# An attention and feed-forward block: products with V in two halves of 64 rows, and the banks shared out anew

## The chip, the cores and the metric

The kernel runs on one core of one Trainium2 chip. The metric is the time of one execution on the device in microseconds (us), as the median of the runs. The core's engines work side by side, each through a list of its own in order: TensorE (PE in the profile, with its weight loads as PEld), VectorE (DVE), ScalarE (ACT), GpSimd (POOL) and SyncE (SP), which here only starts transfers. Matmul results land in PSUM, which has eight banks of 128 partitions x 512 fp32.

## What is computed

One transformer block on x of 2048 x 512 in fp32: 32 query heads of width 16 that share one key head and one value head, then a gated feed-forward part of width 1792.

```python
def _A_ref(x, wq, wk, wv, wo):
    q = (x @ wq).reshape(B, S, H, Dh).transpose(0, 2, 1, 3)
    k = x @ wk
    v = x @ wv
    scores = jnp.einsum("bhqd,bkd->bhqk", q, k) * (Dh ** -0.5)
    p = softmax(scores, axis=-1)
    o = jnp.einsum("bhqk,bkd->bhqd", p, v)
    return o.transpose(0, 2, 1, 3).reshape(B, S, H * Dh) @ wo

def _B_ref(x, w_gate, w_up, w_down):
    return (gelu(x @ w_gate) * (x @ w_up)) @ w_down

h = x + _A_ref(layernorm(x), wq, wk, wv, wo)
h2 = h + _B_ref(layernorm(h), w_gate, w_up, w_down)
```

## The kernel before

**Blocks and groups.** The 2048 query positions are cut into four blocks of 512 (T). Heads go in eight groups of four per block, and keys in 16 chunks of 128. One *step* of attention is one block, one group and one key chunk: 4 x 8 x 16 = 512 steps. A step has two halves (u), each for two heads.

**Scores.** `scores` (line 345) multiplies, for each half, the keys with the queries of two heads. Queries and keys are split into a high and a low part, so that a contraction has 50 rows; the two heads of a half lie in rows 0 to 49 and 64 to 113 of TensorE, which takes both matmuls at once as two tiles of 64 rows. Each writes one bank, so a half needs a pair of banks. One exponential on ScalarE (line 356) then takes the pair, 128 x 1024 elements, into the tile p. There are 1024 halves.

**Products with V.** `weigh` (line 358) runs when both halves of a step have been through the exponential: four calls, one per head, each with all 128 key rows of v_sb and 32 output columns, into four strips of 32 partitions of one accumulator bank, acc. The four strips are four tiles of 128 rows x 32 columns. After 16 chunks `evacuate` (line 371) copies acc to oT on VectorE; the copy then goes through DRAM, is divided by the sums (the upper half of each strip) and becomes the input of the output projection. These are the only products that TensorE takes in full fp32; the others use a rounded fp32 form with explicit high and low parts.

**Dense products.** The output projection, gate, up and down products of blocks 0 to 2 are cut by contraction rows as well: `rows(a)` (line 753) makes two streams, one over rows 0 to 63 and one over rows 64 to 127 of every product, and `step` (line 782) issues one matmul of each. The second stream runs LAG = 6 steps behind the first. A product has 12 matmuls in most cases. At its start a stream takes a bank from the list `spare`, and after the last matmul it gives the bank back to the end of that list and has VectorE read it (`done`: lines 585, 588, 635, 639, 702). The tile framework makes the next writer of a bank wait for the last reader. `queue_products` (line 722) lists the products: for each of blocks 0 to 2 four projections, 28 gate and up products, 8 down products of the runs of features and 4 more, and 4 of the block before where there is one.

**Order of work.** TensorE, ScalarE and GpSimd run in the order written. Three parts matter:

- In the *first stretch* (bank set `ps_first`), block 0's attention runs beside the query projections of the later blocks (`project_q`, line 195). The string PERIOD, played eight times, sets the order: s is a half of scores, v one V step, p a few matmuls of the projection, n a small piece of the same. There are three pairs of score banks: two called s in the pool pss, and a third, s3, for every third half (lines 347 to 349). One bank, d, serves the projections, and one is acc.
- In the *second stretch* (`ps_rest`), from half 279 on, the rounds of CYCLES (line 48) set it. A cycle starts with a burst of three or two V steps (`finish(count)`, line 1102) and then plays a string of s and d, d being a step of the dense streams. Two pairs of score banks, acc, and three dense banks d0, d1, d2 fill PSUM. `turn` (line 593) transposes the normed rows of a block, four transposes into a bank taken from `spare`, which VectorE reads twice.
- The *last part* (`last_dense`, line 818) does block 3's dense work alone, with banks of a new pool (`tail_bank`, line 792) in place of the score banks.

```python
PERIOD = "psssvvssvnsspsssvvssvnssvssvssvvssspssvssvvnsssvvssvss"
LAG = 6
CYCLES = (
    (3, "ssdddddsdddsddds", "vssvssvs"),
    (3, "ssdddddsdddsddds", "vssvssvs"),
    (2, "ssdddddsdddsdddsddds", "ssvssvss"),
)
```

Of the kernel before, what the change touches and what calls it, by code (L numbers as in the profile page):

```python
# [9 lines left out]
F32 = mybir.dt.float32  # L10
# [4 lines left out]
ALU = mybir.AluOpType  # L15
# [4 lines left out]
P = 128  # L20
# [37 lines left out]
def kernel(  # L58
# [12 lines left out]
    nc = tc.nc  # L71
# [6 lines left out]
    T = 512  # L78
    NT = S // P
    NB = S // T  # L80
    TB = T // P
    DC = D // P
    FC = F // P
    NG = H // 4
    KC = S // P
# [25 lines left out]
    v_sb = const.tile([P, KC, 2 * DH], F32, name="v_sb")  # L111
# [9 lines left out]
    def split(eng_hi, hi, lo, src, eng_lo=None):  # L121
        if eng_hi is nc.scalar:
            nc.scalar.activation(hi, src, AF.Copy)
        else:
            eng_hi.tensor_copy(hi, src)
        (eng_lo or nc.vector).tensor_tensor(lo, src, hi.bitcast(F32), op=ALU.subtract)
# [29 lines left out]
    def run(outer, first):  # L156
        banks, held_banks = ExitStack(), ExitStack()
        ps = pss = None
# [6 lines left out]
        width = 0  # L165

        def psum1(name):
            if not spare:
                return ps.tile([P, T], F32, tag="d", bufs=width, name=name)
            tag, bank = take_bank(name)  # L170
            spare.append(tag)
            return bank

        spare = []

        def take_bank(name):
            tag = spare.pop(0)
            return tag, ps.tile([P, T], F32, tag=tag, bufs=1, name=name)
# [143 lines left out]
        if first:  # L322
            set_banks("ps_pro")
            width = 8
# [19 lines left out]

        def scores(i, p, qg, kc, u):

            third = width == 1 and (2 * i + u) % 3 == 2
            pool, tag, bufs = (ps, "s3", 1) if third else (pss, "s", 2)
            s = pool.tile([P, 2, T], F32, tag=tag, bufs=bufs, name=f"s_{i}_{u}")
            for a in range(2):  # L350
                rows = slice(64 * a, 64 * a + KR)
                nc.tensor.matmul(  # L352
                    s[:, a, :], kaug[rows, kc * P : (kc + 1) * P], qg[rows, u, :],
                    start=True, stop=True,
                )
            nc.scalar.activation(p[:, 2 * u : 2 * u + 2, :], s, AF.Exp, scale=SCALE)  # L356

        def weigh(acc, p, kc):
            for j in range(4):
                nc.tensor.matmul(  # L360
                    acc[32 * j : 32 * j + 32, :], v_sb[:, kc, :], p[:, j, :],
                    start=(kc == 0), stop=(kc == KC - 1), skip_group_check=True,
                )

        def take_out():
            for step in outs.pop(0):
                step()

        def evacuate(b, g, acc):
            oT = sb.tile([P, T], F32, tag="oT", bufs=1, name=f"oT_{b}_{g}")
            nc.vector.tensor_copy(oT, acc)  # L373
            c, k = divmod(g, 2)
            if k == 0:
                pair[0] = sb.tile([P, 2, T], F32, tag="oc", bufs=2, name=f"oc_{b}_{c}")
            oc = pair[0]

            def move_out():
                for half in (1, 0):  # L380
                    for j in range(4):
                        r0, r1 = 64 * k + DH * j, 32 * j + DH * half
                        (nc.sync, nc.scalar)[j % 2].dma_start(
                            oc[r0 : r0 + DH, half, :], oT[r1 : r1 + DH, :]
                        )

            def turn_out():
                view = acc_d[:, g % 4, :].rearrange("(j s e) t -> j e s t", s=2, e=DH)
                for j in range(4):
                    r0 = 64 * k + DH * j  # L390
                    nc.sync.dma_start(oc[r0 : r0 + DH, :, :], view[j])


            def invert(t):
                sl = slice(t * P, (t + 1) * P)
                nc.vector.reciprocal(oc[:, 1, sl], oc[:, 1, sl])  # L396

            def divide():
                if c == 0:
                    o_blk[b] = [  # L400
                        sb.tile([P, DC, T], F32R, tag=f"o_{w}", bufs=1, name=f"o_{w}_{b}")
                        for w in ("hi", "lo")
                    ]
                hi, lo = o_blk[b]
                nc.vector.tensor_tensor(oc[:, 0, :], oc[:, 0, :], oc[:, 1, :], op=ALU.mult)
                split(nc.vector, hi[:, c, :], lo[:, c, :], oc[:, 0, :])


            def piece(t):
                sl = slice(t * P, (t + 1) * P)  # L410
                hi, lo = o_blk[b]
                invert(t)
                nc.vector.tensor_tensor(
                    oc[:, 0, sl], oc[:, 0, sl], oc[:, 1, sl], op=ALU.mult
                )
                split(nc.vector, hi[:, c, sl], lo[:, c, sl], oc[:, 0, sl])
                pieces[b] = t + 1

            if b == NB - 1 and g == NG - 1:
                move_out()  # L420
            else:
                nc.sync.dma_start(acc_d[:, g % 4, :], oT)
                if b == 0 and g < NG - 1:
                    outs.append([turn_out])
                else:
                    turn_out()
            if b == NB - 1 and g == NG - 1:
                last_out.append(piece)
            elif b > 0 and g == NG - 1:
                outs.extend([partial(piece, t), partial(piece, t + 1)] for t in (0, 2))  # L430
            elif k == 1:

                outs.extend([[] for _ in range(4 if b == 0 else 1)])
                outs.extend([partial(invert, t), partial(invert, t + 1)] for t in (0, 2))
                outs.append([divide])
            if b == 0 and g == NG - 1:
                while outs:
                    take_out()
                pieces[b] = TB
# [97 lines left out]
        def new_xT(b):  # L537
            xTs[b] = [
                db.tile([P, DC, T], F32R, tag=f"x2{w[0]}", bufs=1, name=f"x2{w[0]}_{b}")
                for w in ("hi", "lo")  # L540
            ]
# [49 lines left out]
            return f"pp_{b}_{t}", 3 * DC, terms, done, lambda: pieces.get(b, 0) > t  # L591

        def turn(b, t):
            tag, bank = take_bank(f"pxt_{b}_{t}")
            pt = bank.rearrange("p (c q) -> p c q", c=DC)
            xn = xbs.pop((b, t))
            for c in range(DC):
                nc.tensor.transpose(pt[:, c, :], xn[:, c * P : (c + 1) * P], ident)
            if b not in xTs:
                new_xT(b)  # L600
            sl = slice(t * P, (t + 1) * P)
            hi, lo = (x[:, :, sl] for x in xTs[b])
            nc.vector.tensor_copy(hi, pt)
            nc.vector.tensor_tensor(lo, pt, hi.bitcast(F32), op=ALU.subtract)
            spare.append(tag)
            load_x(b * TB + t + 3)
            turned[b] = t + 1

# [181 lines left out]
                ahead -= 1  # L790

        def tail_bank(name):
            return tail_ps.tile([P, T], F32, tag="t", bufs=5, name=name)

        tail_ps = None

# [21 lines left out]
        def last_dense():  # L818
            b = NB - 1
# [5 lines left out]
            def x_turn(t):  # L825
# [9 lines left out]
            xp, xn, h = (  # L835
                sb.tile([P, TB, D], F32, tag="p", bufs=PB, name=f"{n}p_{b}")
                for n in ("x", "xn", "h")
            )
# [2 lines left out]
            for j in range(2):  # L841
                load_w2(b, j)

            pps = [psum1(f"pp_{b}_0")]
            pps.extend(tail_bank(f"pp_{b}_{t}") for t in range(1, TB))

            def add_x(t):
                nc.tensor.matmul(pps[t], ident, xp[:, t, :], start=False, stop=False)
# [108 lines left out]
        acc = None  # L957
# [17 lines left out]
        def score(n):  # L975

            nonlocal acc
            i, u = divmod(n, 2)
            b, r = divmod(i, PER)
            g, kc = divmod(r, KC)  # L980
            if u == 0:
                if kc == 0:
                    cur["qg"] = qgs.pop((b, g))
                    acc = pss.tile([P, T], F32, tag="acc", bufs=1, name=f"acc_{b}_{g}")
                if kc == 2 and b * NG + g + 1 < NB * NG:
                    key = divmod(b * NG + g + 1, NG)
                    qgs[key] = load_q(*key)
                cur["p"] = sb.tile([P, 4, T], F32, tag="p", bufs=PB, name=f"p_{i}")
            scores(i, cur["p"], cur["qg"], kc, u)
            if u == 1:  # L990
                pend.append((b, g, kc, cur["p"], acc, n))

        banks.close()
        pss = held_banks.enter_context(
            tc.tile_pool(name="ps_s", bufs=1, side="right", space=PSUM)
        )
        set_banks("ps_first")
        width = 1


        n, lead = 0, 2 * PER + 23
# [55 lines left out]
                    finish(len(pend) - 2)  # L1057
        assert not outs
        set_banks("ps_rest")
        width = 3  # L1060
        spare.extend(f"d{i}" for i in range(width))

        def catch_up():
# [26 lines left out]
        for i in range(-((lead - end) // 16)):  # L1090
# [27 lines left out]
        tail_ps = outer.enter_context(  # L1118
            tc.tile_pool(name="ps_tail", bufs=1, side="right", space=PSUM)
        )  # L1120
# [335 lines left out]
```

## Time and profile before

| What | Value |
|---|---|
| time, median of 2 runs | 1413.44 us (1412.52 to 1414.37) |
| the profiled execution, its own time | 1410.17 us |
| its span in the trace | 1408.5 us |
| granted TensorE clock, mean | 0.999 |
| TensorE busy | 1387.5 us |
| ScalarE busy | 1030.1 us |
| VectorE busy | 630.8 us |

The profile is of one execution, and everything in it is measured from the start of its span. Busy time is time in which an instruction of the engine runs; a matmul's end is modelled, so rows of matmuls overlap, and the distance from start to start tells more than the length of a row. A row of a timeline merges neighbouring instructions of one kind: it gives the first start, the time from there to the last end, and after x the count. What stands in brackets is idle time before the row and what ended it. Waits of TensorE often stand at the weight load (PEld) that comes ahead of the matmul. A matmul in full fp32 leaves two records. A form like 64*128 gives the rows and columns of TensorE that a matmul takes.

### The profile page before, as it was taken

The page shows a single profiled execution, that of the slowest core. Times are in us where ns is not written, and L with a number is a line of the kernel's source. Part 1 is how long each engine was busy: PE and PEld are TensorE (multiplying, and loading weights), DVE is VectorE, ACT ScalarE, POOL GpSimd, SP SyncE. Part 2 cuts the span into 40 slices and gives each one's busy share as a digit, 9 for nine tenths or more (in the row PEclk, how much of TensorE's full clock was granted, in tenths as well). Part 3 has the DMA queues.
Part 4 walks back from the last instruction along what each step waited for, and adds up shares of the span by engine and source line. Part 5 has one row for each costly group of instructions (what it writes and reads, how often), then busy time and mean ns, then how long its engine had stood idle before and what let it go on. Part 6 is the DMA issues. An engine that isn't in the chain of part 4 may idle for free.

```text
span 1408.5 us, 25209 instructions
## 1 busy us (share of the span) xinstructions
PE 1387.5 (99%) x10435; PEld 752.5 (53%) x10435; DVE 630.8 (45%) x1027; ACT 1030.1 (73%) x1147; POOL 222.1 (16%) x321
## 2 busy tenths in 40 slices
PE   8999999999999999999999999999999999999998
PEld 6433333325455555545555555545555555557886
DVE  7411231314364444454354444445264453537665
ACT  7799999997877777877777777777778777752000
POOL 6575777731000000000000000000000000001000
PEclk9999999999999999999999999999999999999999
DMA  4465676745222333321432333311423333344352
GB/s 160 154 198 182 230 243 203 241 137 195 80 95 76 113 113 103 103 71 51 162 104 80 132 102 102 105 62 36 149 95 102 118 102 105 102 142 176 128 191 77
DMA packets 66851, 180.31 MB, mean 128 GB/s; under 512 B 9484, under 2 KB 9484, under 8 KB 66696
## 3 DMA queue, kind: packets, MB, share of 16 engines
q1 hardware_dynamic: 55712, 144.33, 30.8%
q0 software_dynamic: 9760, 34.08, 7.4%
q8 instruction: 84, 1.38, 0.4%
q10 hardware_dynamic: 1256, 0.20, 0.1%
q14 instruction: 39, 0.32, 0.1%
HBM read 130.87 MB, written 47.45 MB: 127 GB/s over the span
## 4 chain that ended last, share of the span: by engine, by line
PE 93%; DMA 2%; ACT 2%; DVE 1%; issue 1%; POOL 0%; SPq 0%; DVEq 0%; ACTq 0%
PE acc L360 33%; PE s L352 20%; PE pg L772 8%; PE pu L772 8%; PE pd L772 8%; PE pq L205 3%; PE pd L802 3%; PE pu L802 3%; PE pg L802 3%; PE pp L772 2%; ACT p L356 2%; DMA w<-w_d 1%; PE pk L1235 1%; DMA x<-in_A_x_dram 1%; PE pd_rest L814 1%
## 5 line engine op out<-in xcount | busy, mean ns | idle before, releaser
L356 ACT ACTIVATE p<-s 128x1024 f32<-128x1024 f32 x1024 | 959.7, 1040 | 227.8 <-PE s L352 225.0
L360 PE MATMUL acc<-p,v_sb 128*32 128x512 f32 x4096 | 490.0, 598 | 0.0
L352 PE MATMUL s<-qg,kaug 50*128 50x512 f32 x1984 | 383.7, 425 | 4.3 <-ACT p L356 4.2
L352 PEld LDWEIGHTS s<-qg,kaug 50*128 50x128 f32 x1984 | 169.5, 184 | 286.6 <-ACT p L356 136.4
L360 PEld LDWEIGHTS acc<-p,v_sb 128*32 128x32 f32 x4096 | 109.9, 109 | 228.6 <-issue 220.5
L772 PE MATMUL pg<-x2h,w 64*128 64x512 f32 x672 | 173.8, 391 | 0.0
L772 PE MATMUL pu<-x2h,w 64*128 64x512 f32 x672 | 172.7, 391 | 0.0
L135 POOL TENSOR_SCALAR rstd<-mv 128x1 f32<-128x1 f32 x16 | 3.5, 219 | 964.2 <-DVE mv L133 964.0
L772 PE MATMUL pd<-w,gh 64*128 64x512 f32 x624 | 123.7, 392 | 1.4 <-DVE h L702 1.4
L702 DVE TENSOR_TENSOR h<-h,pd 128x512 f32<-128x512 f32 x80 | 54.4, 687 | 147.9 <-PE pd L772 147.9
L772 PEld LDWEIGHTS pg<-x2h,w 64*128 64x128 f32 x672 | 94.3, 185 | 12.0
L772 PEld LDWEIGHTS pu<-x2h,w 64*128 64x128 f32 x672 | 94.2, 186 | 11.5
L772 PE MATMUL pg<-x2l,w 64*128 64x512 f32 x336 | 99.3, 391 | 0.0
L772 PE MATMUL pu<-x2l,w 64*128 64x512 f32 x336 | 99.0, 392 | 0.0
L772 PEld LDWEIGHTS pd<-w,gh 64*128 64x128 f32 x624 | 68.1, 185 | 13.1 <-DVE h L702 2.7
L911 ACT ACTIVATE ga<-ga 128x512 f32<-128x512 f32 x14 | 8.8, 632 | 89.6 <-DVE ga L908 89.6
L373 DVE COPY oT<-acc 128x512 f32<-128x512 f32 x32 | 22.1, 691 | 110.7 <-PE acc L360 110.5
L772 PE MATMUL pd<-w,gl 64*128 64x512 f32 x312 | 71.5, 391 | 0.0
L639 DVE TENSOR_TENSOR g<-g,pg 128x512 f32<-128x512 f32 x42 | 28.8, 686 | 90.1 <-PE pg L772 90.1
L396 DVE RECIPROCAL oc<-oc 128x128 f32<-128x128 f32 x64 | 56.6, 922 | 23.3 <-DMA oc<-acc_d 17.5
L635 DVE COPY g<-pg 128x512 f32<-128x512 f32 x42 | 29.1, 692 | 72.0 <-PE pg L772 72.0
L639 DVE TENSOR_TENSOR u<-u,pu 128x512 f32<-128x512 f32 x42 | 28.8, 686 | 68.3 <-PE pu L772 68.3
(247 smaller groups left out, 1465.5 us busy)
## 6 DMA issues: line engine op xcount, KB each, us to landing
w<-w_d SPq DMA_DIRECT2D x112, 512.0 KB
w<-w_d SPq DMA_DIRECT2D x28, 1024.0 KB
qg<-q_d SPq DMA_DIRECT2D x62, 200.0 KB
q_d<-qh SPq DMA_DIRECT2D x32, 256.0 KB
acc_d<-oT SPq DMA_DIRECT2D x31, 256.0 KB
oc<-acc_d SPq DMA_DIRECT2D x124, 64.0 KB
w_d<-w_0b POOLq DMA_DIRECT2D x14, 512.0 KB, 4.3
w_d<-w_1b POOLq DMA_DIRECT2D x14, 512.0 KB, 3.3
```

The lines of the kernel that those rows point to most:

```text
L205: nc.tensor.matmul(pq, wt[c][:, d, :], xt[:, d, :], start=(n == 0), stop=(n == 3 * DC - 1),)
L352: nc.tensor.matmul(s[:, a, :], kaug[rows, kc * P : (kc + 1) * P], qg[rows, u, :], start=True, stop=True,)
L356: nc.scalar.activation(p[:, 2 * u : 2 * u + 2, :], s, AF.Exp, scale=SCALE)
L360: nc.tensor.matmul(acc[32 * j : 32 * j + 32, :], v_sb[:, kc, :], p[:, j, :], start=(kc == 0), stop=(kc == KC - 1), skip_group_check=True,)
L373: nc.vector.tensor_copy(oT, acc)
L396: nc.vector.reciprocal(oc[:, 1, sl], oc[:, 1, sl])
L635: nc.vector.tensor_copy(half, bank)
L639: nc.vector.tensor_tensor(half, half, bank, op=ALU.add)
L702: nc.vector.tensor_tensor(hs[b, t], hs[b, t], bank, op=ALU.add)
L772: nc.tensor.matmul(bank, lhsT[r], rhs[r], start=(k == 0), stop=(k == n - 1), skip_group_check=True,)
L802: nc.tensor.matmul(bank, lhsT, rhs, start=(i == 0), stop=(i == len(ts) - 1))
L814: nc.tensor.matmul(bank, lhsT, rhs, start=(i == 0), stop=(i == len(ts) - 1))
```

## The change

`weigh` makes two calls per head instead of one, on key rows 0 to 63 and 64 to 127, so eight tiles of 64 rows x 32 columns instead of four of 128 x 32. The calls on the upper rows and on the lower rows go into accumulators of their own, acc[0] and acc[1], each one bank. `evacuate` copies the first to oT and adds the second. PSUM's eight banks are shared out anew: the third pair of score banks in the first stretch is gone, and the projections there have two banks (width = 2) instead of one; in the second stretch the dense streams have two banks instead of three, and `turn` takes half of a score pair instead of a dense bank. The last part has six banks in its pool instead of five, and its first projection takes one of these. The strings that set the order, LAG and the list of products stay as they are.

```diff
         def scores(i, p, qg, kc, u):
 
-            third = width == 1 and (2 * i + u) % 3 == 2
-            pool, tag, bufs = (ps, "s3", 1) if third else (pss, "s", 2)
-            s = pool.tile([P, 2, T], F32, tag=tag, bufs=bufs, name=f"s_{i}_{u}")
+            s = pss.tile([P, 2, T], F32, tag="s", bufs=2, name=f"s_{i}_{u}")
...
         def weigh(acc, p, kc):
             for j in range(4):
-                nc.tensor.matmul(
-                    acc[32 * j : 32 * j + 32, :], v_sb[:, kc, :], p[:, j, :],
-                    start=(kc == 0), stop=(kc == KC - 1), skip_group_check=True,
-                )
+                for h in range(2):
+                    half = slice(64 * h, 64 * h + 64)
+                    nc.tensor.matmul(
+                        acc[h][32 * j : 32 * j + 32, :], v_sb[half, kc, :], p[half, j, :],
+                        start=(kc == 0), stop=(kc == KC - 1), skip_group_check=True,
+                    )
...
             oT = sb.tile([P, T], F32, tag="oT", bufs=1, name=f"oT_{b}_{g}")
-            nc.vector.tensor_copy(oT, acc)
+            nc.vector.tensor_copy(oT, acc[0])
+            nc.vector.tensor_tensor(oT, oT, acc[1], op=ALU.add)
...
         def turn(b, t):
-            tag, bank = take_bank(f"pxt_{b}_{t}")
-            pt = bank.rearrange("p (c q) -> p c q", c=DC)
+            bank = pss.tile([P, 2, T], F32, tag="s", bufs=2, name=f"pxt_{b}_{t}")
+            pt = bank[:, 0, :].rearrange("p (c q) -> p c q", c=DC)
...
-            spare.append(tag)
...
         def tail_bank(name):
-            return tail_ps.tile([P, T], F32, tag="t", bufs=5, name=name)
+            return tail_ps.tile([P, T], F32, tag="t", bufs=6, name=name)
...
-            pps = [psum1(f"pp_{b}_0")]
-            pps.extend(tail_bank(f"pp_{b}_{t}") for t in range(1, TB))
+            pps = [tail_bank(f"pp_{b}_{t}") for t in range(TB)]
...
-                    acc = pss.tile([P, T], F32, tag="acc", bufs=1, name=f"acc_{b}_{g}")
+                    acc = [
+                        pss.tile([P, T], F32, tag=f"acc{h}", bufs=1, name=f"acc{h}_{b}_{g}")
+                        for h in range(2)
+                    ]
...
         set_banks("ps_first")
-        width = 1
+        width = 2
...
         set_banks("ps_rest")
-        width = 3
+        width = 2
         spare.extend(f"d{i}" for i in range(width))
```

## Prediction

> **What bounds the kernel now.** I read the page's busy rows first, then the chain, the costliest groups, and then a table of stretches cut where the kernel changes its way of working.
>
> ```profile
> span 1408.5 us, 25209 instructions
> PE 1387.5 (99%) x10435; PEld 752.5 (53%) x10435; DVE 630.8 (45%) x1027; ACT 1030.1 (73%) x1147; POOL 222.1 (16%) x321
> ...
> PE 93%; DMA 2%; ACT 2%; DVE 1%; issue 1%; POOL 0%; SPq 0%; DVEq 0%; ACTq 0%
> ...
> L356 ACT ACTIVATE p<-s 128x1024 f32<-128x1024 f32 x1024 | 959.7, 1040 | 227.8 <-PE s L352 225.0
> L360 PE MATMUL acc<-p,v_sb 128*32 128x512 f32 x4096 | 490.0, 598 | 0.0
> ...
> L373 DVE COPY oT<-acc 128x512 f32<-128x512 f32 x32 | 22.1, 691 | 110.7 <-PE acc L360 110.5
> ```
>
> ```profile
> 49.70:320.50 270.80, 266.94 (x1831) 98.18 (x1831) 64.48 (x91) 260.78 (x279) 173.91 (x213) 1.00 0.64 207
> 320.50:1258.80 938.30, 934.61 (x7747) 507.06 (x7744) 440.48 (x703) 720.23 (x787) 10.08 (x25) 1.00 0.30 102
> ```
>
> The columns of the second fence are stretch, length, then busy us of PE, weight load, DVE, ACT, POOL, then clock and DMA. TensorE works through (99% busy, 93% of the chain), so whatever makes it wait is paid in full. The first stretch (block 0's attention, set ps_first, scores 0 to 279) is bound twice over: TensorE 266.94 and ScalarE 260.78 of 270.80 us. In the second (set ps_rest: attention woven with dense products) ScalarE and VectorE have slack and TensorE has none.
>
> **The change, part by part.** I take the products with V first, then the two exchanges of banks that pay for their second accumulator, then the small edits.
>
> *Products with V.* 2048 calls leave 4096 records, so each fp32 call is two passes. The burst below is three V steps, 24 records, six times four passes side by side.
>
> ```profile
> 687.63 0.40 PE L772 MATMUL pu<-x2h,w 64*128 64x512 f32 x2
> 687.87 0.39 PE L352 MATMUL s<-qg,kaug 50*128 50x512 f32 x2
> 688.19 2.78 PE L360 MATMUL acc<-p,v_sb 128*32 128x512 f32 x24
> 690.90 0.73 PE L352 MATMUL s<-qg,kaug 50*128 50x512 f32 x4
> ```
>
> 490.0 us over 1024 rounds of four is 0.48 with the transitions; I take 0.43 for a pass, six of which are 2.58 of the 2.71 us from burst to score. The change doubles the calls and halves their rows. A pass still streams 512 columns, so nothing is gained if all eight tiles run side by side, and that is my value: 0. A 64-row pass is not shorter as such, which the rows below exclude as a gain: 64-row products follow each other by 0.23 (697.32 to 697.55), 128-row ones by 0.24 (39.08 to 39.32). The loss ends at the two halves running in turn, 512 steps x 0.86 = 440 us; the nearest rows (the paired 64-row products, the four V passes at once) speak for 0.
>
> That the passes may overtake each other is read from the burst: a V step takes two pass times (0.86 us), though each of its four calls holds two passes of one tile in sequence. In strict program order it would take four pass times now (high, low with the next high, and so on) and eight after the change, 512 x 4 x 0.43 = 880 us more. In the Trainium skill, "TensorE: Matmul & The Clock Gate", section "Part 3: Packing small matmuls — row/col tiling", matmuls start and end strictly in program order; by that rule the sum below would be 2565 us, and the trace disagrees with it here (0.86 us a step, not 1.72).
>
> *The transitions.* What the burst pays for entering and leaving: 687.87 to 688.19 is 0.32 against 0.24 between a product and a score; 2.71 against 2.58; and the second score after it comes 0.33 after the first (690.90 + 0.73 - 0.40) instead of 0.24. Together 0.08 + 0.13 + 0.09 = 0.30 us a burst. The code has 8 x 11 bursts in the first stretch and 47 x 3 in the second, 229: 69 us. The change makes the row count alike (64) on both sides and leaves the column count different (32 against 128). Rows where only one of the two differs:
>
> ```profile
> 39.08 0.40 PE L1235 MATMUL pk<-xT_lo,wk_hi 128*128 128x512 f32 x1
> 39.32 0.39 PE L1235 MATMUL pk<-xT_hi,wk_lo 128*128 128x512 f32 x1
> 39.64 0.39 PE L243 MATMUL pqn<-qs,sel 128*32 128x512 bf16 x1
> 39.96 0.50 PE L205 MATMUL pq<-xT_hi,wq_hi 128*128 128x512 f32 x1
> ```
>
> ```profile
> 138.61 0.40 PE L205 MATMUL pq<-xT_hi,wq_lo 128*128 128x512 f32 x1
> 138.93 0.30 PEld L352 LDWEIGHTS s<-qg,kaug 50*128 50x128 f32 x4 [0.36 <-issue]
> 138.93 0.50 PE L352 MATMUL s<-qg,kaug 50*128 50x512 f32 x2
> ```
>
> Columns alone (128 to 32 and back, 39.32, 39.64, 39.96): 0.32 each, against 0.24. Rows alone (138.61 to 138.93): 0.32. Both (687.87 to 688.19): 0.32. The three cost the same, so taking the row half away saves nothing. Value 0, end -69.
>
> *Two dense banks instead of three.* Two streams of products run six steps apart, each holding one bank for 12 matmuls. With three banks the stream that ends a product takes the third. With two, the bank that it just gave back is the only one free, so its next matmul waits for VectorE, and everything behind it on TensorE's queue (the other stream, scores, V) waits too.
>
> ```profile
> 696.88 0.69 DVE L373 COPY oT<-acc 128x512 f32<-128x512 f32 x1 [2.84 <-PE acc L360]
> ...
> 697.32 0.39 PE L772 MATMUL pg<-x2h,w 64*128 64x512 f32 x2
> ...
> 697.55 0.39 PE L772 MATMUL pu<-x2h,w 64*128 64x512 f32 x1
> ...
> 697.74 0.69 DVE L635 COPY g<-pg 128x512 f32<-128x512 f32 x1 [0.17 <-PE pg L772]
> ```
>
> The product pg ends with the matmul of 697.32, its bank is read from 697.74 to 698.43, and the next product pu starts at 697.55 in another bank. One place of this trace already has too few banks:
>
> ```profile
> 933.68 0.39 PE L772 MATMUL pd<-w,gl 64*128 64x512 f32 x2
> 933.91 0.39 PE L772 MATMUL pd<-w,gh 64*128 64x512 f32 x1
> 934.11 1.28 DVE L702 TENSOR_TENSOR h<-h,pd 128x512 f32<-128x512 f32 x2 [3.46 <-PE pd L772]
> 934.85 0.29 PEld L772 LDWEIGHTS pd<-w,gh 64*128 64x128 f32 x3 [0.98 <-DVE h L702]
> 934.85 0.72 PE L772 MATMUL pd<-w,gh 64*128 64x512 f32 x3 [0.55 <-DVE h L702]
> ```
>
> The last matmul starts at 933.68, VectorE at 934.11 (0.43 later), the first of two reads ends near 934.79, the next product starts at 934.85 (0.06 later): 1.17 from the last matmul to the next product, 0.94 more than the usual 0.23. So a handover costs 0.94, and 0.71 where a score (0.23) stands in between.
>
> ```profile
> L702 DVE TENSOR_TENSOR h<-h,pd 128x512 f32<-128x512 f32 x80 | 54.4, 687 | 147.9 <-PE pd L772 147.9
> L635 DVE COPY g<-pg 128x512 f32<-128x512 f32 x42 | 29.1, 692 | 72.0 <-PE pg L772 72.0
> ```
>
> How many: the list holds 3 x (4 + 28 + 8 + 4) + 4 = 136 products, two halves each, 272 handovers (80 of them are the L702 row, 42 the L635 row). A round of the three cycles has 36 steps, so one stream ends products after steps 12, 24 and 36, the other after 6, 18 and 30. Step 36 is followed by a V burst, as 687.63 to 690.90 shows, and that covers the 1.17; step 30 by a score; the other four by the next step. So 5/6 of 272 = 227 handovers at (4 x 0.94 + 0.71)/5 = 0.89: **203 us**. Low end: all at 0.71, 161 us. High end: VectorE is busy 440.48 of 938.30 us, so on average 0.47 x half of 0.69 = 0.16 us more before a read begins, 240 us. I take 203, by the handover that was measured.
>
> *Two pairs of score banks in the first stretch instead of three.* A score waits for the exponential two scores back, not three.
>
> ```profile
> 130.49 0.73 PE L352 MATMUL s<-qg,kaug 50*128 50x512 f32 x4
> ...
> 132.15 0.73 PE L352 MATMUL s<-qg,kaug 50*128 50x512 f32 x4
> ...
> 133.80 0.87 PE L352 MATMUL s<-qg,kaug 50*128 50x512 f32 x4
> ...
> 136.45 0.96 PE L352 MATMUL s<-qg,kaug 50*128 50x512 f32 x6
> ...
> 137.05 2.86 ACT L356 ACTIVATE p<-s 128x1024 f32<-128x1024 f32 x3 [0.18 <-PE s L352]
> ```
>
> An exponential takes 260.78/279 = 0.93 us, and the one after an empty ScalarE starts 0.60 after its score (136.45 to 137.05). Between the last score ahead of other work and the first behind it lie, with 0.40 taken off a row's end for the last start: 1.33 for one V step (130.82 to 132.15), 2.18 for two (134.27 to 136.45), 1.92 for six matmuls of the projection (137.01 to 138.93). Two pairs hold at most 1.86 us of work for ScalarE when TensorE turns away, so ScalarE goes idle for gap + 0.60 - 1.86: 0.07, 0.92, 0.66. Three pairs hold 2.79 and cover all of them (2.18 + 0.60 = 2.78), and ScalarE is indeed busy for 260.78 of 270.80 us now. The order PERIOD has six, five and three of these gaps: 0.4 + 4.6 + 2.0 = 7.0 us, times 8: **56 us**. Low end: only the double V steps cost, 37. High end: all 14 gaps cost 0.92, 103. The value is nearer the low end because the three gap lengths are each measured.
>
> *The small edits.* The read of the accumulator becomes two instructions. The second adds about 0.69 (as L702); in the second stretch it stands ahead of a bank's read: oT at 696.88 would end at 698.26 instead of 697.57, and the read due at 697.74 comes 0.52 later, once per group, 24 groups: **12 us** (end 0, if VectorE was idle there). The next group's V waits for it too, but lies behind scores and a product run. The 12 transposes that move to a score bank hold it for two VectorE reads (1.4 us); the V burst that follows them (2.6) covers that: 0, or 17 uncovered. The second bank of the first stretch saves at most four waits of 0.69: taken as 0. At the end the last group's read stands open once: **1 us**. The sixth bank of the last part: 0, since the waits there are for data.
>
> *Sum.* 203 + 56 + 12 + 1 = 272 us, on the profiled execution's own 1410.2: 1682. The median of the runs, 1413.4, is 3.3 above that execution, so **1685 us**.
>
> **Rivals.** (B) *The transitions go free* with equal row counts: 1685 - 69 = 1616. For it: nothing in the trace has 64-row tiles of two widths. Against it: columns alone cost as much as both. (C) *The halves queue up.* If the upper and the lower tile of a column share one queue, the second half's high pass starts with the first half's low pass, and each burst ends one pass late: 229 x 0.43 = 98, 1783 us. For it: each V call is two passes in sequence, and no row shows two-pass calls in tiles above each other. Against it: 64-row products pair up freely. If the halves ran wholly in turn, 1685 + 440 = 2125. In strict program order, 1685 + 880 = 2565, which the 0.86 us of a step speaks against. (D) *Not slower: TensorE passes a matmul that waits.* Then work of the other stream or a V step fills each handover and each late score, and only the added VectorE work is left, 1413 + 13 = 1426. It decides only if under a tenth of 259 us (203 + 56) stays open, since 28 us is 2%. For it: passes of other tiles overtake within a burst. Against it: at 933.91 to 934.85 the waiting product let nothing else by.
>
> **How the numbers follow.** My forecast, 78%; its own bounds are 1413 + 161 + 37 = 1611 and 1413 + 240 + 103 + 30 = 1786, most of it 1645 to 1725. B 8%, C 8% at 1783 and 3% at 2125, D 2%, strict order and anything else 1%. A range of 1600 to 1790 holds the forecast, B and the milder C. About 2% is what a measurement of this kernel can tell from no change. All cases but D are slower by more than that, so slower 0.97; D is within 2%, 0.02; faster, which needs D and B together, 0.01.
>
> **What would show it.** Right: idle time before dense matmuls released by VectorE's reads (L635, L639, L702 and the pp reads), about 200 us where now there is almost none; the first stretch longer by some 55 us, with waits of scores for ScalarE; V passes still 0.43 apart, eight at a time; the step from score to V still 0.32. Wrong: a V burst of three steps much over 2.7 us (C), scores right behind V at 0.24 (B), or a second stretch still near 938 us (D).

## The result and the profile after

The changed kernel takes 1719.77 us (1718.09 to 1721.45, two runs) against 1413.44: a ratio of 1.2176, 95% interval 1.2152 to 1.2199. It is slower by 306 us; 1685 was forecast, with 1600 to 1790 as the range. The rows below are from the execution of 1721.45 us, whose span is 1719.7.

From the page, busy rows, chain and the two costliest groups of the attention:

```profile
span 1719.7 us, 33475 instructions
PE 1510.6 (88%) x14531; PEld 797.1 (46%) x14531; DVE 656.8 (38%) x1059; ACT 1063.3 (62%) x1147; POOL 221.6 (13%) x321
...
PE 77%; DVE 12%; ACT 8%; issue 2%; DMA 1%; POOL 0%; SPq 0%; ACTq 0%; DVEq 0%
...
L354 ACT ACTIVATE p<-s 128x1024 f32<-128x1024 f32 x1024 | 992.1, 1025 | 504.3 <-PE s L350 504.3
...
L360 PE MATMUL acc<-p,v_sb 64*32 64x512 f32 x8192 | 501.8, 600 | 0.0
```

TensorE was busy for 99% of the span and is now busy for 88%; the chain that ended last, which held 1% of VectorE and 2% of ScalarE, now holds 12% and 8%. The V records have doubled to 8192 and their busy time has hardly moved (490.0 to 501.8). Where the time went by stretch (length, then busy us of PE, weight load, DVE, ACT, POOL; clock and DMA at the end), cut at the same exponentials as before:

```profile
49.90:392.80 342.90, 294.31 (x2941) 105.62 (x2941) 69.33 (x99) 264.52 (x279) 173.14 (x213) 0.98 0.54 175
392.80:1568.50 1175.70, 1027.69 (x10717) 540.88 (x10709) 460.77 (x726) 749.40 (x787) 10.09 (x25) 1.00 0.24 78
```

The first stretch grew from 271 to 343 us, the second from 938 to 1176. ScalarE, which was busy for all but 10 us of the first, now stands idle for 78 of it.

The granted clock was 1.00 in both stretches before. In the changed kernel's trace it stands at one half for 3.4 us at six places of the two stretches (from 52.0, 62.2, 359.2, 372.8, 430.8 and 1185.2), and a V pass takes 0.85 us there instead of 0.43. These 20 us at half clock cost at most 10 of the 306; no run takes them apart from the rest.

**The V steps.** A burst of two steps, from the timeline of TensorE and its weight loads:

```profile
860.44 0.40 PE L350 MATMUL s<-qg,kaug 50*128 50x512 f32 x1
860.76 0.18 PEld L360 LDWEIGHTS acc<-p,v_sb 64*32 64x32 f32 x16 [0.37 <-issue]
860.77 1.95 PE L360 MATMUL acc<-p,v_sb 64*32 64x512 f32 x32
861.22 0.15 PEld L360 LDWEIGHTS acc<-p,v_sb 64*32 64x32 f32 x8 [0.28 <-issue]
861.65 0.15 PEld L360 LDWEIGHTS acc<-p,v_sb 64*32 64x32 f32 x8 [0.28 <-issue]
862.64 0.30 PEld L350 LDWEIGHTS s<-qg,kaug 50*128 50x128 f32 x4 [0.84 <-issue]
862.64 0.74 PE L350 MATMUL s<-qg,kaug 50*128 50x512 f32 x4
```

The weight loads come eight at a time and 0.43 apart (861.22, 861.65): eight tiles run side by side, at the pass time that four had. The way in takes 0.33 (860.44 to 860.77) as before. The way out is 1.87 - 4 x 0.43 = 0.15 us, against 0.13 before, and the second score still comes 0.34 after the first. So equal row counts on both sides bought nothing.

**The handover of a dense bank.** A plain one, and one behind the doubled read of the accumulator:

```profile
869.14 0.60 PE L772 MATMUL pu<-x2h,w 64*128 64x512 f32 x2
869.57 0.69 DVE L635 COPY u<-pu 128x512 f32<-128x512 f32 x1 [0.94 <-PE pu L772]
...
870.31 0.18 PEld L772 LDWEIGHTS pg<-x2h,w 64*128 64x128 f32 x1 [0.99 <-DVE u L635]
870.32 0.49 PE L772 MATMUL pg<-x2h,w 64*128 64x512 f32 x1 [0.57 <-DVE u L635]
...
870.32 0.49 PE L772 MATMUL pu<-x2h,w 64*128 64x512 f32 x1
...
870.65 0.40 PE L350 MATMUL s<-qg,kaug 50*128 50x512 f32 x2
```

```profile
862.80 0.69 DVE L373 COPY oT<-acc 128x512 f32<-128x512 f32 x1 [3.93 <-PE acc L360]
...
863.22 0.39 PE L772 MATMUL pg<-x2h,w 64*128 64x512 f32 x2
863.60 0.69 DVE L374 TENSOR_TENSOR oT<-oT,acc 128x512 f32<-128x512 f32 x1
864.20 0.68 DVE L635 COPY g<-pg 128x512 f32<-128x512 f32 x1
...
864.94 0.18 PEld L772 LDWEIGHTS pu<-x2h,w 64*128 64x128 f32 x1 [1.77 <-DVE g L635]
864.94 0.50 PE L772 MATMUL pu<-x2h,w 64*128 64x512 f32 x1 [1.34 <-DVE g L635]
...
865.28 0.39 PE L772 MATMUL pu<-x2l,w 64*128 64x512 f32 x1
```

In the first, the product's last matmul starts at 869.14, VectorE reads the bank from 869.57, and the weight load of the next product starts at 870.31, 1.17 us after that matmul, to the hundredth what the one case in the old trace had shown. In the second the second read of acc goes first, and it takes 1.72 (863.22 to 864.94), 0.55 more. The weight load stands with the matmul that waits (870.31 and 870.32, both at 864.94), where it otherwise runs during the matmul ahead; so the next matmul comes 0.33 and 0.34 later (870.32 to 870.65, 864.94 to 865.28) instead of 0.23 to 0.24. Summed by the releaser, the waits before the weight loads of the dense products, after:

```profile
L772 PEld LDWEIGHTS pg<-x2h,w 64*128 64x128 f32 x672 | 115.0, 185 | 83.8 <-DVE u L639 29.9 <-DVE u L635 26.2 <-DVE h L702 15.8
L772 PEld LDWEIGHTS pu<-x2h,w 64*128 64x128 f32 x672 | 114.7, 185 | 84.9 <-DVE g L639 38.2 <-DVE g L635 34.3
L772 PEld LDWEIGHTS pd<-w,gh 64*128 64x128 f32 x624 | 80.5, 185 | 78.9 <-DVE h L702 47.5 <-DVE u L639 8.9 <-DVE u L635 7.3
```

and before:

```profile
L772 PEld LDWEIGHTS pg<-x2h,w 64*128 64x128 f32 x672 | 94.3, 185 | 12.0
L772 PEld LDWEIGHTS pu<-x2h,w 64*128 64x128 f32 x672 | 94.2, 186 | 11.5
L772 PEld LDWEIGHTS pd<-w,gh 64*128 64x128 f32 x624 | 68.1, 185 | 13.1 <-DVE h L702 2.7
```

The idle time of these three groups went from 36.6 to 247.6 us, and the releasers named are VectorE's reads of the banks.

**The first stretch.** Rows of TensorE and ScalarE around a double V step:

```profile
140.65 0.19 PEld L350 LDWEIGHTS s<-qg,kaug 50*128 50x128 f32 x2 [1.38 <-ACT p L354]
140.65 0.50 PE L350 MATMUL s<-qg,kaug 50*128 50x512 f32 x2 [0.95 <-ACT p L354]
...
141.08 1.95 PE L360 MATMUL acc<-p,v_sb 64*32 64x512 f32 x32
...
142.96 0.30 PEld L350 LDWEIGHTS s<-qg,kaug 50*128 50x128 f32 x4 [0.84 <-ACT p L354]
142.96 0.73 PE L350 MATMUL s<-qg,kaug 50*128 50x512 f32 x4
143.50 1.94 ACT L354 ACTIVATE p<-s 128x1024 f32<-128x1024 f32 x2 [0.94 <-PE s L350]
```

Both engines wait for each other in turn. The score at 140.65 waits 0.95 us for ScalarE to empty a pair; then TensorE is away with V until 142.96, and ScalarE has nothing from 142.56 to 143.50. From last score to next score it is 2.31 us (140.65 to 142.96), where 2.18 was measured before, since that score's own load had to wait as well.

### The profile page after: what moved, and what is told of

The parts are those of the page before. It is cut to its first block, busy times and chain, and to the rows that moved or that the text cites. A ratio compares the mean times of both kernels' runs of the same rounds, so it can differ in the third digit from the quotient of the medians.

```text
span 1719.7 us, 33475 instructions
## 1 busy us (share of the span) xinstructions
PE 1510.6 (88%) x14531; PEld 797.1 (46%) x14531; DVE 656.8 (38%) x1059; ACT 1063.3 (62%) x1147; POOL 221.6 (13%) x321
## 4 chain that ended last, share of the span: by engine, by line
PE 77%; DVE 12%; ACT 8%; issue 2%; DMA 1%; POOL 0%; SPq 0%; ACTq 0%; DVEq 0%
PE acc L360 25%; PE s L350 15%; PE pg L772 8%; PE pu L772 8%; ACT p L354 7%; PE pd L772 7%; PE pq L205 3%; DVE h L702 3%; PE pd L802 2%; PE pu L802 2%; PE pg L802 2%; PE pp L772 2%; DVE u L639 2%; DVE g L639 2%; DVE u L635 1%
## 5 line engine op out<-in xcount | busy, mean ns | idle before, releaser
L354 ACT ACTIVATE p<-s 128x1024 f32<-128x1024 f32 x1024 | 992.1, 1025 | 504.3 <-PE s L350 504.3
L350 PE MATMUL s<-qg,kaug 50*128 50x512 f32 x1984 | 462.7, 435 | 48.2 <-ACT p L354 43.9
L360 PE MATMUL acc<-p,v_sb 64*32 64x512 f32 x8192 | 501.8, 600 | 0.0
L350 PEld LDWEIGHTS s<-qg,kaug 50*128 50x128 f32 x1984 | 215.0, 185 | 311.9 <-ACT p L354 174.4
L772 PE MATMUL pu<-x2h,w 64*128 64x512 f32 x672 | 214.3, 406 | 43.0 <-DVE g L635 23.0
L772 PE MATMUL pg<-x2h,w 64*128 64x512 f32 x672 | 214.4, 406 | 41.1 <-DVE u L635 16.7
L360 PEld LDWEIGHTS acc<-p,v_sb 64*32 64x32 f32 x8192 | 127.3, 106 | 229.9 <-issue 217.8
L772 PE MATMUL pd<-w,gh 64*128 64x512 f32 x624 | 150.1, 410 | 41.6 <-DVE h L702 27.8
L772 PEld LDWEIGHTS pg<-x2h,w 64*128 64x128 f32 x672 | 115.0, 185 | 83.8 <-DVE u L639 29.9
L772 PE MATMUL pu<-x2l,w 64*128 64x512 f32 x336 | 120.2, 401 | 0.0
```

The costliest lines, as they stand in the source:

```text
L350: nc.tensor.matmul(s[:, a, :], kaug[rows, kc * P : (kc + 1) * P], qg[rows, u, :], start=True, stop=True,)
L360: nc.tensor.matmul(acc[h][32 * j : 32 * j + 32, :], v_sb[half, kc, :], p[half, j, :], start=(kc == 0), stop=(kc == KC - 1), skip_group_che ...
L772: nc.tensor.matmul(bank, lhsT[r], rhs[r], start=(k == 0), stop=(k == n - 1), skip_group_check=True,)
```

## The experiments

The theory after the result: the halves of V are neutral, and the banks given up for the second accumulator carry the loss, in two places that add up. The rival: the doubled V records and their transitions, or the second read, carry a good part. The kernel before took 1411.55 us beside e1 to e4 (7 runs) and 1411.31 beside e5 to e8 (7 runs). The lengths of the stretches in the table run from exponential 1 to 280 and from there to the last, in each run's trace.

| Kernel | us, median of 4 | ratio to before (95%) | first | second |
|---|---|---|---|---|
| before (profiled execution) | 1410.17 | | 270.7 | 936.4 |
| changed kernel (profiled execution, 1721.45) | 1719.77 | 1.2176 (1.2152 to 1.2199) | 342.8 | 1173.6 |
| e1, banks only | 1702.93 | 1.2066 (1.2043 to 1.2088) | 339.7 | 1158.4 |
| e2, banks of the first stretch | 1478.96 | 1.0466 (1.0443 to 1.0489) | 339.8 | 938.5 |
| e3, banks of the second stretch | 1638.67 | 1.1605 (1.1583 to 1.1627) | 272.3 | 1162.2 |
| e4, no second read | 1708.35 | 1.2110 (1.2083 to 1.2138) | 338.3 | 1163.4 |
| e5, changed, aligned | 1540.17 | 1.0911 (1.0893 to 1.0929) | 340.0 | 994.7 |
| e6, before, aligned | 1433.05 | 1.0148 (1.0131 to 1.0165) | 272.5 | 955.6 |
| e7, changed, single V steps | 1706.05 | 1.2079 (1.2058 to 1.2099) | 325.9 | 1175.9 |
| e8, changed, both orders | 1525.10 | 1.0805 (1.0783 to 1.0827) | 326.0 | 994.1 |

(The first two rows hold the measurements of the result; the changed kernel's time is the median of two runs.)

**e1: the exchange of banks alone.** The changed kernel with V as it was:

```diff
         def weigh(acc, p, kc):
             for j in range(4):
-                for h in range(2):
...
+                nc.tensor.matmul(
+                    acc[32 * j : 32 * j + 32, :], v_sb[:, kc, :], p[:, j, :],
...
-            nc.vector.tensor_copy(oT, acc[0])
-            nc.vector.tensor_tensor(oT, oT, acc[1], op=ALU.add)
+            nc.vector.tensor_copy(oT, acc)
```

> The changed kernel's banks (two dense banks, two score pairs, transposes in a score bank), but V again in one call of 128 rows into one accumulator with one read. Theory (the exchange of banks carries the loss, the halves cost little): 1700 to 1715 us, since only the second read of the accumulator and some 5 us of slower exits from V leave. Rival (the doubled V records and their transitions carry a good part): well below 1650 us; if they carried all of it, 1413 us.

It took 1702.93 us: without any half of V in it, the kernel loses 291 of the 306 us. The theory holds, the rival falls.

**e2: the first stretch's banks alone.** The kernel before with two pairs of score banks:

```diff
-            third = width == 1 and (2 * i + u) % 3 == 2
-            pool, tag, bufs = (ps, "s3", 1) if third else (pss, "s", 2)
-            s = pool.tile([P, 2, T], F32, tag=tag, bufs=bufs, name=f"s_{i}_{u}")
+            s = pss.tile([P, 2, T], F32, tag="s", bufs=2, name=f"s_{i}_{u}")
...
-        width = 1
+        width = 2
```

> The kernel before with only the first stretch's banks exchanged (two score pairs throughout, two projection banks). Theory: the first stretch grows from 271 to about 340 us and the rest stays, so 1413 + 70 = 1483 us. Rival (the first stretch grew because of the halves or the second read): 1413 to 1425 us.

1478.96 us, 67 more than before, and by the stretches all of it in the first (339.8 against 270.7; second 938.5 against 936.4).

**e3: the second stretch's banks alone.** The kernel before with two dense banks; the transposes and the last part follow as in the change:

```diff
-            tag, bank = take_bank(f"pxt_{b}_{t}")
-            pt = bank.rearrange("p (c q) -> p c q", c=DC)
+            bank = pss.tile([P, 2, T], F32, tag="s", bufs=2, name=f"pxt_{b}_{t}")
+            pt = bank[:, 0, :].rearrange("p (c q) -> p c q", c=DC)
...
-            spare.append(tag)
...
-        width = 3
+        width = 2
```

> The kernel before with only the second stretch's banks exchanged (two dense banks, transposes in a score bank, six banks in the last part). Theory: the second stretch grows from 937 by the handovers, 203 us as forecast plus 0.1 us for each weight load that now waits too (23 us), so 1413 + 226 = 1639 us, 1625 to 1650. Rival (handovers cost less, the halves and the second read make up the second stretch's 237 us): under 1590 us.

1638.67 us, 227 more, again in its own stretch (1162.2 against 936.4). 67 + 227 = 294 against the 291 of e1: the two places add up. e3 moves the transposes into a score bank as well; in its trace scores wait 3.7 us for VectorE's second read of them (x2l).

**e4: without the second read.** `nc.vector.tensor_tensor(oT, oT, acc[1], op=ALU.add)` is left out of the changed kernel.

> The changed kernel without the second read of the accumulator: acc[1] is computed and never added, so half of the key rows are missing from the output. Theory (that read stands ahead of a dense bank's read once per group and in front of V): 10 to 15 us less than the changed kernel, 1705 to 1710 us. Rival (VectorE has room for it): 1720 us. If the read were behind the excess over the forecast, 1685 us.

1708.35 us, 11 less than the changed kernel; in the profiled executions the second stretch is 10 us shorter and the first 4 to 5. e1 lies 17 below the changed kernel, so some 5 us are left for the halves themselves. That is what the way out makes: over all bursts that a score follows its median is 0.157 us in the changed kernel and 0.134 before, and 0.023 us at each of the 243 bursts that the traces hold comes to 5.6.

**e5 and e6: the handover moved under the V bursts.** Both streams end their products on the last dense step of a cycle; e5 is the changed kernel, e6 the kernel before:

```diff
-LAG = 6
+LAG = 12
...
-    (3, "ssdddddsdddsddds", "vssvssvs"),
-    (3, "ssdddddsdddsddds", "vssvssvs"),
-    (2, "ssdddddsdddsdddsddds", "ssvssvss"),
+    (3, "ssdddddsddddsddds", "vssvssvs"),
+    (3, "ssdddddsddddsddds", "vssvssvs"),
+    (2, "ssdddsdddsdddsddds", "ssvssvss"),
```

> The changed kernel with LAG 12 and 12 dense steps in each cycle, so that both streams end their products on the last step ahead of a V burst. Theory (the loss of the second stretch is the wait of a product for its own bank, 1.17 us after its last matmul): a burst of 2.7 us covers it for both streams, the second stretch falls from 1174 to 950 to 985 us, and the total to 1500 to 1535 us. Rival (two dense banks cost whatever the order, by reads that queue on VectorE): over 1650 us.

> The kernel before with the same order (LAG 12, 12 dense steps a cycle), as a control. Theory: its third bank hides the handover in any order, 1405 to 1425 us. Rival (the order itself is better or worse): more than 15 us away from 1412.

e5 took 1540.17 us, 5 above the expected band: the second stretch fell by 179 us, to 994.7, 10 above its own. e6 took 1433.05, so the order is not neutral; it costs 22 us where three banks hide the handover anyway, outside what was expected. Measured against its own control, the changed kernel's second stretch is 39 us longer (994.7 against 955.6) where it was 237 longer in the old order. The timeline of e5 shows the cover:

```profile
861.29 0.39 PE L772 MATMUL pd<-w,gl 64*128 64x512 f32 x1
861.30 0.39 PE L772 MATMUL pu<-x2h,w 64*128 64x512 f32 x1
...
861.52 0.39 PE L350 MATMUL s<-qg,kaug 50*128 50x512 f32 x2
861.72 0.69 DVE L702 TENSOR_TENSOR h<-h,pd 128x512 f32<-128x512 f32 x1 [1.74 <-PE pu L772]
...
861.85 2.81 PE L360 MATMUL acc<-p,v_sb 64*32 64x512 f32 x48
...
862.33 0.68 DVE L639 TENSOR_TENSOR u<-u,pu 128x512 f32<-128x512 f32 x1
...
864.58 0.73 PE L350 MATMUL s<-qg,kaug 50*128 50x512 f32 x4
...
865.15 0.62 PE L772 MATMUL pd<-w,gh 64*128 64x512 f32 x4
```

Both streams end at 861.3, VectorE is through with both banks at 863.01, and TensorE, which had three V steps to do until 864.58, starts the next products at 865.15 without a wait. So the same banks and the same reads cost 39 us instead of 237 once something else lies behind a product's end. Part of these 39 us is seen in the trace of e5, as waits for VectorE on TensorE:

```profile
L350 PE MATMUL s<-qg,kaug 50*128 50x512 f32 x1984 | 410.9, 439 | 59.0 <-ACT p L354 49.9 <-DVE x2l L605 8.8
...
L772 PE MATMUL pd<-w,gh 64*128 64x512 f32 x624 | 130.2, 398 | 9.9 <-DVE h L702 9.9
```

Scores wait 8.8 us for the second read of the transposes (x2l), which now share the score banks, and down products 9.9 us for their banks. Most of what the order itself costs in e6 is late scores: its scores wait more for ScalarE (12.6 against 4.2 us before their matmuls on TensorE), and from start to start 51 of them behind other matmuls than V lose 19 us, where 9 lost 4 before.

**e7 and e8: no double V steps in the first stretch.** e7 is the changed kernel with PERIOD changed, e8 is e5 with the same:

```diff
-PERIOD = "psssvvssvnsspsssvvssvnssvssvssvvssspssvssvvnsssvvssvss"
+PERIOD = "psssvsvsvnsspsssvsvsvnssvssvssvsvsspssvssvsvnssvsvsvss"
```

> The changed kernel with no two V steps in a row in the first stretch: vvss becomes vsvs in PERIOD. Theory (two score pairs hold 1.86 us of exponentials, which a double V step outlasts by 0.9 us and a single one does not): 5 x 0.85 us saved and 5 x 0.30 us of transitions added in each of eight periods, so the first stretch falls from 343 to about 321 us and the total to about 1698 us. Rival (the stretch is slow for another reason than the long gaps): 1720 us or more, by the added transitions 1732.

> The changed kernel with both orders, the aligned dense products and the single V steps. Theory: the savings add up, since they lie in different stretches: 1720 - 200 - 22 = about 1498 us, 1475 to 1515. Rival (they share a cause): no better than the better one of the two alone.

e7 took 1706.05 us, with a first stretch of 325.9 instead of 342.8: the long gaps do cost, and splitting them wins back 17 of the 22 us expected in it; the total fell by 14 and lies 8 above the forecast. e8 took 1525.10, with a first stretch of 326.0 and a second of 994.1, just those of e7 and e5. The total lies 10 us above the band, since both parts won less than was expected of them. The savings add up: 180 and 14 us alone, 195 together. No version with two accumulators beat the kernel before; the best of them, e8, takes 8% longer.

## Why the prediction was right, point by point

- *Products with V, 0 us.* Right. Eight tiles run at once, passes stay 0.43 apart, and neither milder nor harsher form of rival C showed up (way in and passes as before, the way out 0.02 longer). Strict program order, which would have come to 2565 us, is out too.
- *Transitions, 0 us.* Close: 0.33 in, as before, and 0.15 instead of 0.13 out, some 5 us in all where none was expected. Rival B is out. The argument held that columns alone cost as much as rows and columns together.
- *Handovers of the dense banks, 203 us.* The mechanism was right, the size 10% short: e3 measured 227. The count was good: the trace of e3 has 220 weight loads of dense products that wait over 0.2 us for a read by VectorE, where 227 were forecast. So was the price: for 214 of them the read had itself waited for the product's last matmul, and they come 1.16 to 1.24 us after that matmul. What was missed is that the weight load waits with its matmul, so that the matmul after comes 0.10 us late; 227 handovers make that 23 us (24 counted in the trace of e3), and 203 + 23 = 226. The prediction's own rows showed it: the row at 934.85 holds three matmuls and lasts 0.72, so the last of them starts 0.33 after the first. That the sum meets the 227 so closely is partly luck, since the 227 also hold the transposes, which were put at 0, and 17 us at half clock, which cost at most 9.
- *Score banks, 56 us.* The mechanism was right, the size short: e2 measured 67, and the changed kernel's first stretch grew by 72. Exponentials in a row start 0.905 us apart; what an exponential starts later than that is counted here as idle time of ScalarE. In the changed kernel's trace it is 1.32 us on average at the 40 double V steps (0.92 was forecast), 0.95 at the 24 sets of six projection matmuls (0.66) and 0.10 at the 52 single V steps (0.07): 53 + 23 + 5 = 81 us, with about 8 in other places; before, the same count gives 18, so it finds 71 of the 72. The mis-sized term is what two pairs hold when TensorE turns away. It was taken as two full exponentials of 0.93, but they come 0.905 apart, the last score starts only after the one before the last has ended, and its late load stretches the gap from 2.18 to 2.31. The clock, at half for 14 us of this stretch, can have added at most 7.
- *Second read, 12 us.* Right: 11 by e4, and 0.55 us where it stands ahead of a handover (0.52 was taken).
- *Rival D, TensorE passing a matmul that waits,* is out: the second matmul of the row at 869.14 starts at 869.36, and nothing else starts until 870.31.

The sum with the measured terms: 67 + 227 + 11 + 5 = 310, against 306 measured. The forecast of 1685 lies 35 us below, and the handovers and the score banks carry that: 24 and 11 us by e3 and e2.

## What to carry to other kernels

Count what a PSUM bank does before giving it away: where an in-order engine goes from one product straight to the next, a stream with no spare bank pays the reader's whole latency at each product (here 1.17 us instead of 0.23, plus 0.10 for the weight load that waits too). If banks must go, change the order with them, so that each product ends ahead of other long work; here that took back 179 of 237 us. A change meant to make one attribute of neighbouring matmuls equal should first be checked against a pair of rows that differ in the other attribute alone.

## What the runs showed of the hardware

Eight tiles of 64 x 32, each with a two-pass fp32 product, run side by side at the 0.43 us a pass of four tiles of 128 x 32, into two banks at once. Leaving them for 64 x 128 took 0.02 us longer than leaving 128 x 32, which was not expected. In these kernels the weight load of a matmul that waits for another engine waits as well, and the start after it comes 0.10 us late (0.33 to 0.34 instead of 0.23 to 0.24). The granted clock falls to one half for some 3.4 us at a time in the changed kernel, which it did not do in these stretches before; what makes it fall was not tested.
